# ReLU² attention and ReLU² MLP on one core: an earlier k load, a re-laid start of the MLP, two units' copies moved to VectorE, and a planner with shorter visits

## The chip, the cores and the metric

The kernel runs on one core of one Trainium2 chip. The metric is device time of one execution in microseconds (us). Nine runs of the kernel before had a median of 378.81 us and lay between 378.26 and 379.09 us. One further record is a profiled execution, whose instruction times are quoted throughout.

## The reference

The inputs are q, k and v of shape (8 batches, 12 heads, 448 rows, 64) and two weight matrices, all float32. What is computed:

```python
scores = (1/8) * q @ k.transpose
attn   = maximum(scores, 0)**2 / 448
x      = (attn @ v), heads side by side: 3584 tokens x 768
h      = x @ w_in                      # 768 -> 2048
g      = maximum(h, 0)**2
out    = g @ w_out                     # 2048 -> 768
```

There is no softmax, so a tile of attn needs only a relu with a scale (done by ScalarE out of PSUM) and a square (done by VectorE in SBUF).

## The kernel before

**Engines.** TensorE does all products, ScalarE (ACT) the relus of the scores and many evacuations of PSUM, VectorE (DVE) the squares, sums and other evacuations. GpSimd (POOL) issues the loads, which convert to float16 on the way; SP issues the DMA transposes and most stores. Each engine works through its instructions in the order in which the Python code emits them (`manual_schedule`).

**Attention.** Each batch is cut into three *units* of four heads (24 units in all), and each unit into seven *tiles* of 64 score columns per head (tile t belongs to unit t // 7). `score(t)` runs four 64x64 matmuls into a PSUM *slot*, and one ScalarE relu (line 256) empties it into an `at` tile, which VectorE squares (line 369). Two slots rotate, and a third exists in the first rounds only. When all seven tiles of a unit are squared, attn x v follows. For batch 0 this is `av_round`, tile by tile (line 270). For later units it is `av_unit`: 28 matmuls (line 317) and one ScalarE copy into `xt` (line 323).

**q and k, transposed.** Scores need q and k with the head dimension on the partitions. Units 0 to 5 are loaded as they are (`load16`) and transposed on TensorE by `pe_transpose(n)`: 28 small matmuls (line 222) into one slot, and two copies out of it, qT and kT. ScalarE makes these copies at line 214, VectorE at line 216: before the change VectorE for units 0 to 2, ScalarE for units 3 to 5. The slot is not free until both copies are done. Units 6 and up are transposed by DMA (`prefetch`).

**Visits.** A `visit` scores two tiles and queues their squares. In the first stage, 11 visits do the 21 tiles of batch 0, with each score run twice (`score(t, 2)`). After that, visits are *events*: each has a due time on a clock that only the matmul steps of the MLP advance, and it is emitted at the first step marked as an edge at which its time has come.

**MLP.** Batches 0 and 1 take plain products. `h_group(b, f)` is six matmuls of 448 columns (line 420, 0.1892 us each on the clock, so T_G = 1.135 us a group), then a relu by VectorE (line 429; batch 0, f = 0 and odd f below 14) or ScalarE (line 433), then `flush()`, which emits all squares that wait; after every odd group VectorE squares two columns of g (line 439). T_H, 16 groups, is the clock time at which batch 1 begins. Batches 2 to 7 (`h_period`, line 550) and the second product (`o_groups`, line 729) form 2x2 blocks with seven products instead of eight. They need sums of blocks, made by VectorE: `sums_w2` and `sums_w1` of the weights (lines 151 and 178 to 184), `sums_x`, and `sums` of g (line 602, called s1 to s4 below).

**The planner.** From batch 2 on, and in the second product, the order of VectorE's work comes from a model made while the code is emitted. `at_pe` is where TensorE would be, `at_ve` where VectorE would be. Squares go into a queue `due`, the relu and square of g into `due_g`, each with a time from which it is ready. `fill(until)` emits queued work that the model finishes before `until`; `now_ve(cost)` books an instruction that is emitted at once; `flush` empties the queues. `av_unit` flushes `due` ahead of its matmuls. A visit of two tiles counts as 0.19 + 0.38 * 2 = 0.95 us of TensorE, an `av_unit` as 2.65 us. These two figures change the order of VectorE's instructions alone: TensorE's steps follow the other clock.

**The seam.** Visit 11 scores tile 20, transposes unit 3 and does two tiles of attn x v. Then come four matmuls of group f = 0 (they need only units 0 and 1), the last three tiles of attn x v of batch 0, the first visit of batch 1, and the rest of the groups.

Of the kernel before, what the change touches and what calls it, by code (L numbers as in the profile page):

```python
# [12 lines left out]
AF = mybir.ActivationFunctionType  # L13
# [4 lines left out]
def kernel(  # L18
# [71 lines left out]
    def load16(n):  # L90
        tq = q16_p.tile([P, 2, J * D], FP16, name="q16", tag="q16")
        tk = q16_p.tile([P, 2, J * D], FP16, name="k16", tag="k16")
        nc.gpsimd.dma_start(out=tq, in_=heads(q, n))
        nc.gpsimd.dma_start(out=tk, in_=heads(k, n))
        q16s[n] = (tq, tk)

    def load_v(n):
        t = v_p.tile([P, 2, J * D], FP16, name="vt", tag="vt")
        nc.gpsimd.dma_start(out=t, in_=heads(v, n))
        vts[n] = t  # L100
# [44 lines left out]
    def sums_w2(i):  # L145


        op, c = divmod(i, 2)
        c = slice(4 * c, 4 * c + 4)
        dst, x, y = ((t1, b12, b11), (t3, b22, b12), (t2, b22, t1), (nt4, b21, t2))[op]  # L150
        nc.vector.tensor_sub(dst[:, c], x[:, c], y[:, c])
# [5 lines left out]
    nc.vector.memset(zeros, 0.0)  # L157
    junk = const_p.tile([P, 1], FP16, name="junk", tag="junk")
    nc.scalar.activation(out=junk, in_=zeros[:, 0:1], func=AF.Relu)
    load_v(0)  # L160
    load16(1)
    load_v(1)
    load16(2)
    load_v(2)

    def sums_w1(i):


        op, c = divmod(i, 2)
        now_ve(0.9)  # L170
        lo, hi = slice(0, NM // 2), slice(NM // 2, NM)
        a11, a12, a21, a22 = (w1[c][:, lo], w1[c][:, hi], w1[c + 2][:, lo],
                              w1[c + 2][:, hi])
        if op < 3:
            wsum[op, c] = late["ws"].tile(
                [P, NM // 2, 512], FP16, name=f"ws{op}{c}", tag=f"ws{op}{c}")
        if op == 0:
            nc.vector.tensor_add(wsum[0, c], a21, a22)
        elif op == 1:
            nc.vector.tensor_sub(wsum[1, c], wsum[0, c], a11)  # L180
        elif op == 2:
            nc.vector.tensor_sub(wsum[2, c], a12, wsum[1, c])
        else:
            nc.vector.tensor_sub(a21, a11, a21)
# [21 lines left out]
    def pe_transpose(n):  # L206
        srcs = q16s.pop(n)
        ts = new_qkt()
        ps = slot(FP16)

        def copy(i, eng):
            dst = ts[i].rearrange("p j c -> p (j c)")
            if eng == 0:
                nc.scalar.activation(out=dst, in_=pss[i][:, i, 0:J * P], func=AF.Copy)  # L214
            else:
                nc.vector.tensor_copy(dst, pss[i][:, i, 0:J * P])

        pss = [ps, slot(FP16) if n == 0 else ps]
        for i, src in enumerate(srcs):
            for j in range(J):  # L220
                for hh in range(2):
                    nc.tensor.transpose(  # L222
                        pss[i][64 * hh:64 * hh + 64, i, j * P:(j + 1) * P],
                        src[:, hh, j * D:(j + 1) * D], ident)
            if n == 0:
                copy(i, 1)
                warm(1)
        qkt[n] = ts
        if n == 3:
            return lambda: (copy(0, 0), copy(1, 0))  # L230
        if n > 0:
            copy(0, n < 3)
            copy(1, n < 3)
        return None


    xts: dict = {}
# [63 lines left out]
    def av_unit():  # L301

        n = unit[0]
        if n == NUN or seen.get(n * J + J - 1, 10 ** 6) >= now[0]:
            return
        unit[0] += 1
        flush(rest=False)
        at_pe[0] += 2.65
        b, u = divmod(n, NU)
        vt = vts[n]  # L310
        ps = slot(FP32)
        for j in range(J):
            at = ats.pop(n * J + j)
            for hp in range(2):
                r = slice(64 * hp, 64 * hp + 64)
                for hh in range(2):
                    nc.tensor.matmul(  # L317
                        ps[64 * hh:64 * hh + 64, hp, 0:S],
                        lhsT=vt[r, hh, j * D:(j + 1) * D], rhs=at[r, hh, :],
                        start=(j == 0), stop=(j == J - 1))  # L320
        if u == 0:
            xts[b] = x_p.tile([P, NM, S], FP16, name="xt", tag="xt")
        nc.scalar.activation(
            out=xts[b][:, 2 * u:2 * u + 2, :], in_=ps[:, :, 0:S],
            func=AF.Copy, scale=CX)
# [34 lines left out]
    def now_ve(cost, lag=0.25):  # L360
        at_ve[0] = max(at_ve[0], at_pe[0] + lag) + cost
# [9 lines left out]
    def visit(tiles, turn=None, lag=2, most=3):  # L371
        now[0] += 1
        for t in tiles:
            if t % J == 0 and t >= NPE * J:
                prefetch(t // J + 2)
        if big:
            for t in tiles[:1]:
                score(t)
            av_unit()
            for t in tiles[1:]:  # L380
                score(t)
            at_pe[0] += 0.19 + 0.38 * len(tiles)
            for i, t in enumerate(tiles):
                square(ats[t], 0.6 + 0.85 * i)
            return
        for t in tiles:
            score(t, 2)
        later = pe_transpose(turn) if turn is not None else None
        flush()
        av_some(lag, most)  # L390
        if later:
            later()
        for t in tiles:
            square(ats[t])
        flush()
# [16 lines left out]
    def h_group(b, f):  # L412
        z = (b % 2) * S
        cell = [None]

        def step(m):
            def run():
                if m == 0:
                    cell[0] = mm_tile()
                nc.tensor.matmul(  # L420
                    cell[0][:, 0:S],
                    lhsT=w1[f // 4][:, m, (f % 4) * P:(f % 4 + 1) * P],
                    rhs=xts[b][:, m, :], start=(m == 0), stop=(m == NM - 1))
                if m < NM - 1:
                    return
                f0 = f - f % 2
                g = g_of(b)[:, f0:f0 + 2, z:z + S]
                if b == 0 and (f % 2 == 1 or f == 0) and f < 14:
                    nc.vector.tensor_scalar(
                        out=g[:, f % 2], in0=cell[0][:, 0:S],  # L430
                        scalar1=0.0, scalar2=None, op0=ALU.max)
                else:
                    nc.scalar.activation(
                        out=g[:, f % 2], in_=cell[0][:, 0:S], func=AF.Relu)
                flush()
                if b == 0 and f == NF - 1:
                    square(g)
                elif f % 2 == 1:
                    nc.vector.tensor_mul(g, g, g)
            return run  # L440

        return [(0.1892, step(m), m == 0) for m in range(NM)]
# [151 lines left out]
    def sums(i, rows, to):  # L594

        a1, a2 = tile_of(rows[0]), tile_of(rows[1])
        x, y = ((a2[:, LO], a2[:, HI]), (to.get(1), a1[:, LO]),
                (a1[:, LO], a2[:, LO]), (a1[:, HI], to.get(2)))[i - 1]
        to[i] = late["s"].tile([P, KH, P], FP16, name=f"s{i}", tag=f"s{i}")
        op = nc.vector.tensor_add if i == 1 else nc.vector.tensor_sub  # L600
        now_ve(0.6)
        op(to[i], x, y)  # L602

# [170 lines left out]
    warm(10)  # L774
    pe_transpose(0)
    for i in range(11):
        visit([t for t in (2 * i, 2 * i + 1) if t < NB0],
              turn={1: 1, 4: 2, 10: 3}.get(i))
        if i == 0:
            load16(3)  # L780
            load_w1(0)
            load_w1(1)
            load_v(3)
        if i == 2:
            load16(4)
            load_w1(2)
            load_v(4)
        if i == 5:
            load16(5)
            load_w1(3)  # L790
            load_v(5)
    load_v(6)
    load_w2(b11, 0, 0)
    load_w2(b12, 0, 1)
# [2 lines left out]
    load_qk(6)  # L797
    load_qk(7)
    first.close()
    big.append(ctx.enter_context(tc.tile_pool(name="mma", bufs=2, space=PSUM)))  # L800


    f0 = h_group(0, 0)
    for _, fn, _ in f0[0:4]:
        fn()
    av_some(0, 9)
    rounds.close()
    big.append(ctx.enter_context(tc.tile_pool(
        name="mmb", bufs=2, space=PSUM, side="right", reuse_waits="tile")))
    visit([NB0, NB0 + 1])  # L810

    T_G = NM * 0.1892
# [20 lines left out]

    events.append((T_H + 0.2, ready))
    for i in range(8):
        events.append((T_H + (1 + i // 2) * T_G, lambda i=i: sums_w2(i)))
    for i in range(6):
        events.append((T_H + (8 + i) * T_G, lambda i=i: sums_w1(i)))
    for i in range(2):
        events.append((2 * T_H + 3 + 3 * i, lambda i=i: sums_w1(6 + i)))  # L840
    for m in (6, 7):
# [33 lines left out]
    for i in (1, 2):  # L875
        events.append((2 * T_H - (3 - i) * T_G, lambda i=i: outs[0][1](i)))

    steps = [(0.1892, None, False)] * 4 + f0[4:]
    for f in range(1, NF):
        steps += h_group(0, f)  # L880
    for f in range(NF):
        steps += h_group(1, f)
# [49 lines left out]
```

## Time and profile before

| | before |
|---|---|
| median of 9 runs | 378.81 us |
| the profiled execution's own time | 379.09 us |
| its span, first to last instruction | 377.3 us |
| TensorE matmul busy | 362.8 us (96%) |
| VectorE busy | 277.8 us (74%) |
| ScalarE busy | 249.8 us (66%) |
| GpSimd busy | 107.3 us (28%) |
| granted TensorE clock | 0.999 |

The span starts with the first instruction. 1.8 us of the profiled time lie outside it. Busy time of TensorE covers the whole passage of each matmul, so back-to-back matmuls overlap in it. The stages, by the start of their first matmul: transposes from 5.18 us, attention of batch 0 from 7.60, MLP groups of batch 0 from 27.69, the last attn x v of batch 1 (unit 5) at 58.76 and groups of batch 1 from about 61.6, the first second product from 84.11, then alternating `h_period` and `o_groups` to the last matmul at 372 us.

How lines of the views read: in a timeline, "12.35 4.96 ACT L256 ... x6 [0.79 <-PE slot L252]" means that from 12.35 us, for 4.96 us, ScalarE ran six instructions of line 256, and was idle for 0.79 us before them until TensorE's line 252 released it. In the list of waits, the three figures are total us, times, and the longest.

### The profile page before, as it was taken

How to read it: one execution, taken by the hardware profiler on the slowest of the kernel's cores; microseconds unless marked ns; L12 is line 12 of the kernel's file. 1: busy time of each engine (PE TensorE's matmuls, PEld its weight loads, DVE VectorE, ACT ScalarE, POOL GpSimd, SP SyncE). 2: the span in 40 equal slices, each digit the busy share in tenths (PEclk: the TensorE clock that was granted, in tenths of full speed). 3: DMA queues.
4: the chain of work that ended last, by engine and by line, in shares of the span. 5: the costliest groups of instructions: out<-in, count | busy, mean ns of one | idle time of the engine just before them, and what ended most of it. 6: DMA issues, size and time to landing. Idle time of an engine off the chain costs nothing.

```text
span 377.3 us, 8806 instructions
## 1 busy us (share of the span) xinstructions
PE 362.8 (96%) x3600; PEld 231.0 (61%) x3600; DVE 277.8 (74%) x515; ACT 249.8 (66%) x373; POOL 107.3 (28%) x128
## 2 busy tenths in 40 slices
PE   7889999999999999999999999999999999999994
PEld 3544444444455778785555577877555588985663
DVE  1886567997767688797865758989957688995542
ACT  2897995686777798775566578877766785532220
POOL 8545431927422436404041344050000000000001
PEclk9999999999999999999999999999999999999999
DMA  8999999999999999679498997693232200002333
GB/s 116 201 204 205 205 203 156 131 150 148 142 131 164 153 144 143 76 94 79 96 112 134 194 169 79 74 105 66 40 95 77 70 25 2 2 0 64 94 95 86
DMA packets 121160, 42.65 MB, mean 113 GB/s; under 512 B 100832, under 2 KB 117760, under 8 KB 121120
## 3 DMA queue, kind: packets, MB, share of 16 engines
q0 software_dynamic: 82912, 23.01, 60.6%
q1 hardware_dynamic: 38048, 18.98, 27.2%
q8 instruction: 28, 0.46, 0.5%
q14 instruction: 12, 0.10, 0.1%
q10 hardware_dynamic: 160, 0.10, 0.1%
HBM read 45.61 MB, written 11.01 MB: 150 GB/s over the span
## 4 chain that ended last, share of the span: by engine, by line
PE 82%; ACT 6%; DVE 6%; issue 2%; DMA 2%; POOL 1%; POOLq 0%; ACTq 0%; DVEq 0%
PE mm L729 33%; PE mm L550 23%; PE slot L252 9%; PE mm L420 9%; PE slot L317 7%; ACT at L256 4%; DVE at L369 2%; DMA k<-in_k_dram 2%; PE slot L222 1%; DVE g L491 1%; ACT m L486 1%; DVE xt L283 1%; DVE s L602 1%; DVE g L498 0%; ACT qT L214 0%
## 5 line engine op out<-in xcount | busy, mean ns | idle before, releaser
L256 ACT ACTIVATE at<-slot 128x896 f16<-128x896 f32 x168 | 146.1, 919 | 32.7 <-PE slot L252 32.7
L369 DVE TENSOR_TENSOR at<-at 128x896 f16<-128x896 f16 x168 | 99.8, 618 | 15.9 <-ACT at L256 14.8
L108 POOL DMA_DIRECT2D qs<-in_q_dram x36 | 35.3, 983 | 120.0 <-DMA qT<-qs 112.3
L729 PEld LDWEIGHTS <-s 128*128 128x128 f16 x440 | 41.7, 98 | 32.0 <-issue 4.3
L252 PE MATMUL slot<-qT,kT 64*64 64x448 f16 x756 | 58.1, 360 | 2.6 <-ACT at L256 1.2
L550 PEld LDWEIGHTS <-w 128*128 128x128 f16 x576 | 54.4, 98 | 5.9 <-issue 5.4
L550 PE MATMUL mm<-xt,w 128*128 128x224 f16 x432 | 48.6, 259 | 0.0
L729 PEld LDWEIGHTS <-g 128*128 128x128 f16 x336 | 31.5, 98 | 24.0 <-issue 5.0
L550 PEld LDWEIGHTS <-ws 128*128 128x128 f16 x432 | 40.2, 98 | 6.7 <-issue 6.7
L729 PE MATMUL mm<-b,g 128*128 128x384 f16 x224 | 40.7, 326 | 0.0
L420 PE MATMUL mm<-xt,w 128*128 128x448 f16 x192 | 39.6, 353 | 0.3 <-ACT xt L280 0.3
L729 PE MATMUL mm<-b,s 128*128 128x384 f16 x216 | 39.6, 326 | 0.1
L729 PE MATMUL mm<-t,s 128*128 128x384 f16 x224 | 39.5, 326 | 0.0
L636 DVE SCALAR_TENSOR_TENSOR osb<-mm,u 128x384 f32<-128x384 f32 (+1 forms) x30 | 16.2, 542 | 31.2 <-ACT u L631 23.0
L252 PEld LDWEIGHTS <-kT 64*64 64x64 f16 x756 | 20.0, 104 | 31.0 <-issue 25.7
L108 POOL DMA_DIRECT2D ks<-in_k_dram x36 | 35.3, 981 | 10.1 <-DMA b<-in_moe_w_out_dram 5.8
L571 POOL DMA_DIRECT2D out_dram<-osb x2 | 1.1, 563 | 120.4 <-DVE osb L636 120.4
L631 ACT ACTIVATE u<-mm 128x384 f32<-128x384 f32 x28 | 13.8, 492 | 32.6 <-PE mm L729 31.4
L550 PE MATMUL mm<-x,ws 128*128 128x224 f16 x288 | 34.4, 259 | 0.9 <-ACT m L486 0.9
L317 PE MATMUL slot<-at,vt 64*64 64x448 f16 x588 | 32.2, 350 | 0.6 <-DVE at L369 0.5
L498 DVE TENSOR_TENSOR g<-g 128x896 f16<-128x896 f16 x48 | 29.7, 619 | 1.1 <-ACT g L501 0.2
L420 PEld LDWEIGHTS <-w 128*128 128x128 f16 x192 | 17.3, 98 | 19.1 <-issue 4.8
(66 smaller groups left out, 398.4 us busy)
## 6 DMA issues: line engine op xcount, KB each, us to landing
out_dram<-osb SPq DMA_DIRECT2D x52, 192.0 KB, 3.3
vt<-in_v_dram POOLq DMA_DIRECT2D x24, 224.0 KB, 6.3
qs<-in_q_dram POOLq DMA_DIRECT2D x36, 112.0 KB, 4.8
ks<-in_k_dram POOLq DMA_DIRECT2D x36, 112.0 KB, 5.2
w<-in_moe_w_in_dram POOLq DMA_DIRECT2D x8, 384.0 KB, 12.0
b<-in_moe_w_out_dram POOLq DMA_DIRECT2D x4, 768.0 KB, 17.3
q<-in_q_dram POOLq DMA_DIRECT2D x6, 224.0 KB, 8.1
k<-in_k_dram POOLq DMA_DIRECT2D x6, 224.0 KB, 8.4
```

The source lines that it names most:

```text
L108: nc.gpsimd.dma_start(out=t[:, :, hh, :], in_=heads(src, n)[:, hh].rearrange("p (j d) -> p j d", d=D))
L222: nc.tensor.transpose(pss[i][64 * hh:64 * hh + 64, i, j * P:(j + 1) * P], src[:, hh, j * D:(j + 1) * D], ident)
L252: nc.tensor.matmul(ps[c, hh, 0:S], lhsT=kT[r, j, c], rhs=qT[r, :, c], start=True, stop=True)
L256: nc.scalar.activation(out=at, in_=ps[:, :, 0:S], func=AF.Relu, scale=SK)
L317: nc.tensor.matmul(ps[64 * hh:64 * hh + 64, hp, 0:S], lhsT=vt[r, hh, j * D:(j + 1) * D], rhs=at[r, hh, :], start=(j == 0), stop=(j == J - 1))
L369: lambda: nc.vector.tensor_mul(at, at, at), 0))
L420: nc.tensor.matmul(cell[0][:, 0:S], lhsT=w1[f // 4][:, m, (f % 4) * P:(f % 4 + 1) * P], rhs=xts[b][:, m, :], start=(m == 0), stop=(m == NM ...
L498: due_g.append((t, 0.54, lambda: nc.vector.tensor_mul(g, g, g), b))
L550: nc.tensor.matmul(XY[s][y][:, r * Q:(r + 1) * Q], lhsT=left(k, i0 + 2 * s + r, m), rhs=right(k, m), start=(fresh and r == 0 and m == 0), ...
L631: nc.scalar.activation(out=t, in_=X[0][:, 0:HALF], func=AF.Copy, scale=CO)
L636: nc.vector.scalar_tensor_tensor(out=osb[row][:, c], in0=acc[0][:, 0:cc.stop - cc.start], scalar=CO, in1=keep[nm][:, cc], op0=ALU.mult, op ...
L729: nc.tensor.matmul(acc[0][:, 0:HALF], lhsT=left()[:, f], rhs=right[:, f], start=(fresh and f == 0), stop=(f == KH - 1), skip_group_check=n ...
```

## The change

It does the following.

1. The first loads are issued as q and k of unit 1, v of unit 0, q and k of unit 2, v of units 1 and 2. Before, v of unit 0 came first and v of unit 1 between units 1 and 2.
2. `pe_transpose(3)` leaves visit 11 and comes right after it. Around the rest of attn x v of batch 0, the order is now: tiles 18 and 19, two matmuls of f = 0, the two copies of unit 3 (qT by ScalarE, kT by VectorE), tile 20, two more matmuls of f = 0, two of f = 1, the first visit of batch 1, and then the remaining matmuls of f = 1 and f = 0. The pool of the first two accumulators takes `reuse_waits="tile"`.
3. For units 4 and 5, VectorE makes both copies, after a `flush()`.
4. The planner counts 0.19 us a tile (0.57 for a visit of two) and 1.33 us an `av_unit`. Ahead of each `sums`, squares that the model takes as ready are emitted first.
5. `sums_w2(i)` is due at T_H + (2 + 0.75 i) T_G where it was T_H + (1 + i // 2) T_G; `sums_w1(i)` at T_H + (9 + 0.8 i) T_G where it was T_H + (8 + i) T_G.

```diff
@@ the first loads
+    load16(1)
     load_v(0)
-    load16(1)
+    load16(2)
     load_v(1)
-    load16(2)
     load_v(2)
...
@@ pe_transpose
         qkt[n] = ts
         if n == 3:
-            return lambda: (copy(0, 0), copy(1, 0))
+            return lambda: (copy(0, True), copy(1))
         if n > 0:
-            copy(0, n < 3)
-            copy(1, n < 3)
-        return None
+            flush()
+            copy(0)
+            copy(1)
...
@@ av_unit
-        at_pe[0] += 2.65
+        at_pe[0] += 1.33
...
@@ visit
-            at_pe[0] += 0.19 + 0.38 * len(tiles)
+            at_pe[0] += 0.19 + 0.19 * len(tiles)
...
-        later = pe_transpose(turn) if turn is not None else None
+        if turn is not None:
+            pe_transpose(turn)
         flush()
         av_some(lag, most)
-        if later:
-            later()
...
@@ sums
+        while due and due[0][0] <= max(at_ve[0], at_pe[0]) + 0.3:
+            put(due)
         now_ve(0.6)
         op(to[i], x, y)
...
@@ the seam
-        visit([t for t in (2 * i, 2 * i + 1) if t < NB0],
-              turn={1: 1, 4: 2, 10: 3}.get(i))
+        visit([t for t in (2 * i, 2 * i + 1) if t < NB0], turn={1: 1, 4: 2}.get(i))
...
+    later = pe_transpose(3)
     load_v(6)
...
-    big.append(ctx.enter_context(tc.tile_pool(name="mma", bufs=2, space=PSUM)))
+    big.append(ctx.enter_context(tc.tile_pool(
+        name="mma", bufs=2, space=PSUM, reuse_waits="tile")))
...
-    f0 = h_group(0, 0)
-    for _, fn, _ in f0[0:4]:
-        fn()
+    f0, f1 = h_group(0, 0), h_group(0, 1)
...
+    av_some(1, 9)
+    some(f0[0:2])
+    later()
     av_some(0, 9)
     rounds.close()
...
+    some(f0[2:4])
+    some(f1[0:2])
     visit([NB0, NB0 + 1])
...
-        events.append((T_H + (1 + i // 2) * T_G, lambda i=i: sums_w2(i)))
+        events.append((T_H + (2 + 0.75 * i) * T_G, lambda i=i: sums_w2(i)))
...
-        events.append((T_H + (8 + i) * T_G, lambda i=i: sums_w1(i)))
+        events.append((T_H + (9 + 0.8 * i) * T_G, lambda i=i: sums_w1(i)))
...
-    steps = [(0.1892, None, False)] * 4 + f0[4:]
-    for f in range(1, NF):
+    steps = [(0.1892, None, False)] * 6 + f1[2:4] + f0[4:6] + f1[4:6]
+    for f in range(2, NF):
         steps += h_group(0, f)
```

More of the change, by code (lines that the diff above doesn't have):

```diff
@@ L209, in pe_transpose, with copy @@
         ps = slot(FP16)
[L211 to L214, printed above, removed]
+        def copy(i, act=False):
+            dst, ps = ts[i].rearrange("p j c -> p (j c)"), pss[i][:, i, 0:J * P]
+            if act:
+                nc.scalar.activation(out=dst, in_=ps, func=AF.Copy)
             else:
-                nc.vector.tensor_copy(dst, pss[i][:, i, 0:J * P])
+                nc.vector.tensor_copy(dst, ps)
         pss = [ps, slot(FP16) if n == 0 else ps]
@@ L225, in pe_transpose @@
             if n == 0:
-                copy(i, 1)
+                copy(i)
                 warm(1)
@@ L799, with some @@
     first.close()
-    big.append(ctx.enter_context(tc.tile_pool(name="mma", bufs=2, space=PSUM)))
-    f0 = h_group(0, 0)
-    for _, fn, _ in f0[0:4]:
-        fn()
+    big.append(ctx.enter_context(tc.tile_pool(
+        name="mma", bufs=2, space=PSUM, reuse_waits="tile")))
+    f0, f1 = h_group(0, 0), h_group(0, 1)
+    def some(part):
+        for _, fn, _ in part:
+            fn()
+    av_some(1, 9)
+    some(f0[0:2])
+    later()
     av_some(0, 9)
```

## The prediction

> **What bounds the kernel.** I read the page first: shares, then slices.
>
> ```profile
> PE 362.8 (96%) x3600; PEld 231.0 (61%) x3600; DVE 277.8 (74%) x515; ACT 249.8 (66%) x373; POOL 107.3 (28%) x128
> ...
> PE   7889999999999999999999999999999999999994
> ```
>
> TensorE is the bound, and only its idle time is to be had: 14.5 us of the 377.3, about 5 of them after the last matmul. The change takes no matmul away. So I asked next for whom TensorE waits:
>
> ```profile
> PE slot L222 <- DMA k<-in_k_dram: 0.9, 2, 0.6
> ...
> PE mm L550 <- ACT m L486: 0.9, 3, 0.4
> ...
> PE mm L550 <- DVE g L491: 0.7, 2, 0.3
> ...
> PE slot L252 <- ACT kT L214: 0.5, 2, 0.3
> PE slot L317 <- DVE at L369: 0.5, 2, 0.4
> ```
>
> No wait is large; each edit has to be followed to its own wait. The timelines of the stages that are touched (TensorE, ScalarE and VectorE rows):
>
> ```profile
> 11.22 0.58 PE L222 MATMUL slot<-ident,k 128*64 128x128 f16 x14 [0.64 <-DMA k<-in_k_dram]
> ...
> 12.35 4.96 ACT L256 ACTIVATE at<-slot 128x896 f16<-128x896 f32 x6 [0.79 <-PE slot L252]
> ...
> 26.28 0.58 PE L222 MATMUL slot<-ident,q 128*64 128x128 f16 x14 [0.57 <-ACT at L256]
> ...
> 29.94 2.81 PE L420 MATMUL mm<-xt,w 128*128 128x448 f16 x14 [0.25 <-ACT xt L280]
> ...
> 34.53 0.62 DVE L429 TENSOR_SCALAR g<-mm 128x448 f16<-128x448 f32 x1 [1.13 <-PE mm L420]
> 35.08 1.15 DVE L369 TENSOR_TENSOR at<-at 128x896 f16<-128x896 f16 x2
> 36.14 0.61 DVE L439 TENSOR_TENSOR g<-g 128x896 f16<-128x896 f16 x1
> ...
> 35.44 0.92 ACT L214 ACTIVATE qT<-slot 128x896 f16<-128x896 f16 x1 [0.49 <-PE slot L222]
> 36.26 0.91 ACT L214 ACTIVATE kT<-slot 128x896 f16<-128x896 f16 x1
> ...
> 37.22 0.38 PE L252 MATMUL slot<-qT,kT 64*64 64x448 f16 x4 [0.26 <-ACT kT L214]
> ```
>
> Up to 27 us ScalarE sets the pace (0.82 us from one relu of line 256 to the next), from 28 us on TensorE does, with short waits for slots. The VectorE rows matter most: after a group with odd f (here f = 3) it has four instructions in hand, g, two squares and g squared, before it could copy anything.
>
> **Part 1, the loads.** Transfers land one after the other: q and k of unit 0 at 5.13 and 6.26 us, v of unit 0 at 8.20, q and k of unit 1 at 9.32 and 11.18, then v at 12.26. With v moved behind, q of unit 1 takes v's place (8.20) and k lands at 9.32, or at 10.15 if the long step of 1.86 us belongs to it. The transposes of q run 10.00 to 10.41 (they wait for a slot), those of k follow to 10.90, tile 4's score ends at 10.90 + 0.57 = 11.47. The relu of tile 3 starts at 10.63, so the next can start at 10.63 + 0.82 = 11.45: 11.5 instead of 12.35, **-0.85**. The three issues swap places in GpSimd's queue, 0.7 each, with no wait among them before 11.46. v lands at 11.18, and its first reader (line 270, 12.51 before) comes at 11.7. v of units 1 and 2 lands at 14.6 and 15.7, used at 19 and 24. The stage is paced by ScalarE up to 27 us, so the shift is carried on whole; later loads keep their places and have over 1 us of slack at every reader. Bounds: 0 (another wait takes its place) and -0.9 (all of the gap).
>
> **Part 2, the seam.** Times from here on are those of before, part 1 left out. The two tiles of attn x v of visit 11 (8 matmuls, 0.37 us) come ahead of the transposes and so fall into the 0.57 us wait for a slot, which still ends at 26.28. After the transposes (27.19): 0.50 (tiles 18, 19) + 0.48 (2 matmuls of f = 0) + 0.22 (tile 20) + 0.86 (4) + 0.50 (visit) + 2.37 (12 matmuls to the end of f = 2) = 4.93, so 32.12; before it was 32.68. The wait of 0.25 for xt at 29.94 goes because four matmuls cover it. VectorE's kT copy runs from 27.7 to 28.3, behind the square of tile 20, and the visit needs it at 29; the accumulators of f = 0 were not waited for before, so `reuse_waits` is put at nothing. **-0.56**; bounds -0.2 (one new wait, for the kT copy, at the first visit) and -0.8 (both idles).
>
> **Part 3, copies of units 4 and 5.** TensorE waits in the second score of the next visit for the slot to come free. Before: f = 3 ends at 34.43, transposes 0.91, two ScalarE copies, score at 37.22, 2.74 to the last copy's end at 37.17. After, counted from the same end: 0.10 to the start of g, 0.55 + 1.06 + 0.54 for g, two squares and g squared (the starts above), 0.54 for qT and 0.62 for kT = 3.41. `flush()` adds nothing, since each group has flushed. So +0.66 a unit: in exchange ScalarE is relieved of 1.63 us, and the next visit no longer waits for its relus (tiles 27 and 28: 0.82 from start to start against 0.50 for a visit without a wait, -0.32). Followed through: -0.56 at the end of f = 3; +0.10 at the score; -0.24 at the end of f = 7; unit 5 the same, +0.40 at its score; -0.32, +0.08. There the last squares of unit 4 end 3.40 us after f = 9, while TensorE would now reach the seventh tile of `av_unit` after 3.07: the 0.32 comes back, +0.40. So **+0.96** for part 3, and parts 2 and 3 together +0.40.
> The Trainium skill speaks for this edit: "ScalarE: Activation LUTs", Rules for kernel authors, has VectorE rather than ScalarE for simple element-wise work, and "Perfetto Trace Analysis", Optimizing Scalar/DVE Operations, says a VectorE mode makes it faster, but not where VectorE is saturated. By the first alone, each pair of copies would end earlier and the part would gain. The rows decide: a copy takes 0.62 us at line 216 against 0.92 at line 214, but it stands fifth in its queue.
> Bounds: VectorE free when the transposes end, 35.44 + 0.54 + 0.62 = 36.60 against 37.17, so -0.57 a unit and -0.3 for the relieved visit, -1.7 in all; and +1.5 if no visit is relieved.
>
> **Part 4, sums of the weights.** From 62.4 us VectorE is the fuller engine:
>
> ```profile
> 62.40:86.00 23.60, 23.29 (x35) 1.00 1.73 143
> ```
>
> (of 23.60 us, 23.29 busy). Its row at 62.97 is `sums_w2`, two of the eight, 0.87 each, emitted at group 1. After the change the first stands at group 2, behind the square of groups 0 and 1, which needs ScalarE's relu (64.06 + 0.54 = 64.60). So VectorE stands idle from 62.97 to 64.62, 1.65 us, and everything behind it up to the square of tile 48 (same work, save s1) ends 1.65 later. The `av_unit` of unit 6 starts at 82.50 and needs tile 48 at 83.63; that square ended at 83.31, 0.32 ahead. The new rule in `sums` lets it go ahead of s1 (0.60): the planner has `at_ve` ahead by two bookings of 0.9 at group 13. 1.65 - 0.32 - 0.60 = **+0.73**. Who waits behind it: s1 and s2, 0.6 each, needed only at 88. Bounds: 0 (TensorE late by other causes) and +1.33 (s1 first).
>
> **Part 5, the planner.** The trace has 0.50 us for a visit and 1.32 for 28 matmuls, so the new figures are the truer ones; VectorE looks fuller to the model, and squares and `due_g` go out later, evacuations earlier. What there is to win: the waits for `DVE g L491` stand behind a ScalarE copy that has two relus in front of it, not behind a square (152.57, two relus; 154.18 m; 154.77 g). Of the waits for `DVE at L369`, the large one (0.92 us lost at 92.2) has its squares behind an evacuation emitted before any `fill` could place them; that order stays. About 0.3 is to be won. To lose: read from the rows, 5 of the 17 later units have their last square less than 1 us ahead of need. Two squares left to the flush in `av_unit` take 1.07 from TensorE's arrival, and it needs the last after 0.21 + 1.12 = 1.33; one evacuation of 0.62 in front costs 0.36. Two such cases: **+0.2** net. Bounds -0.5 and +2.0 (six units at 0.36).
>
> **Sum.** -0.85 - 0.56 + 0.96 + 0.73 + 0.2 = +0.48. The profiled execution took 379.09 (377.3 span and 1.8 around it), so 379.57; it stands 0.28 above the median of 378.81, so 379.3. 0.2% is 0.76 us, about what a measurement of this kernel can tell from no change.
>
> **Rivals.** *The lead is kept* (faster): VectorE reaches the two copies as the transposes end, part 3 at -1.7, or the stall of part 4 is covered. For it: ScalarE's copies are on the chain that ends last, and its relus wait behind them. Against it: the four VectorE rows above. With part 3 at 0 and part 4 at 0, -0.85 - 0.56 + 0.2 = -1.2, so 377.6; with part 3 at its bound, 375.9. It decides once kT's copy ends before about 36.5 on the times of before.
> *Squares come late* (slower): the truer planner leaves the last two squares of a unit to the flush in `av_unit`. For it: the small margins; against it: `fill` takes squares ahead of `due_g`. At 0.36 to 0.6 for eight units, +3 to +5 less what part 5 had: about 382. It overtakes the rest from three units on.
> *Nothing reaches the end*: later stages wait for ScalarE anyway (121.85, 150.90, 220.66, 237.38 and 253.09 have ScalarE as releaser), but these waits are fixed to TensorE's steps, so a shift passes through them whole. Time as before, 378.8.
>
> **How the numbers follow.** The sum as worked out, 0.50: range 378.3 to 380.3, so 0.02 faster, 0.28 same, 0.20 slower. The kept lead, 0.26: 0.24 faster, 0.02 same. Late squares, 0.17: all slower. Nothing, 0.07: same. Together faster 0.26, same 0.37, slower 0.37. 377.5 leaves out the lower part of the kept lead, 381.0 most of the late squares, one in ten each.
>
> **What would show it.** Part 1: no 0.79 in front of the third visit's relus, first MLP matmul of f = 2 over 0.8 us earlier. Part 2: no waits at the transposes of unit 3 beyond 0.25 and none for xt. Part 3: VectorE copies directly behind line 439, TensorE idle over 0.5 us in front of two scores, released by kT. Part 4: VectorE idle after 63 us, TensorE waiting for line 369 in unit 6. Wrong would be: kT's copies ahead of the squares, no stall at unit 6, or several new stalls at line 317 after 100 us.

## The result and the profile after

The changed kernel has a median of 380.68 us over 9 runs (380.56 to 380.91), against 378.60 us for the kernel before on the same chip (29 runs; the 378.81 quoted ahead is the median of the first nine): slower by 2.08 us, a ratio of 1.0056 with a 95% interval from 1.0047 to 1.0064. Its profiled execution took 380.60 us with a span of 378.8 us, so the two profiled executions differ by 1.5 us, 0.5 less than the medians. The kernel before's profiled execution (379.09) lies at the top of its runs, the changed kernel's (380.60) near the middle of its own; all that follows about places is read between these two traces.

In the changed kernel the line numbers of the MLP are one lower (L419, L549) or one higher (L730, L603) than before. The page's busy times, and the list of whom TensorE waits for (total us, times, longest):

```profile
PE 363.7 (96%) x3600; PEld 231.0 (61%) x3600; DVE 281.6 (74%) x520; ACT 245.9 (65%) x368; POOL 107.2 (28%) x128
```

```profile
PE slot L252 <- DVE kT L216: 2.3, 3, 0.9
PE slot L317 <- DVE at L369: 1.4, 4, 0.6
...
PE mm L549 <- ACT m L485: 0.9, 3, 0.4
...
PE mm L730 <- DVE s L603: 0.2, 1, 0.2
```

ScalarE did five instructions fewer and VectorE five more. The waits for k's load and for ScalarE's kT are gone from the list. At its head stand VectorE's kT copies (before: 0.4 for one) and squares that attn x v waits for (before: 0.5, twice); a wait for a sum s is new. The waits behind ScalarE's m copies are what they were, 0.9.

The surest way to read where time went is to pair every matmul of one trace with the same matmul of the other, and to see where the difference of their start times changes. There are seven such places (the figures are running totals):

| place | difference after minus before |
|---|---|
| third visit, 11 us | -0.85 |
| end of the seam (visit of tiles 23 and 24) | -1.30 |
| second score behind unit 4's transposes | -0.64 |
| second score behind unit 5's transposes | -0.01 (-0.06 at the next attn x v, -0.01 from 52 us on) |
| unit 6, last tile of attn x v | +0.80 |
| product with s3, 212.7 us | +1.18 |
| unit 20, last tile of attn x v | +1.55, kept to the end |

So the lead of 1.30 us was real, and lost by 47 us. Timelines of the changed kernel at these places. First TensorE and VectorE behind group f = 3, with the transposes of unit 4 ending at 34.03:

```profile
33.23 0.62 DVE L428 TENSOR_SCALAR g<-mm 128x448 f16<-128x448 f32 x1 [0.37 <-PE mm L419]
33.78 1.15 DVE L369 TENSOR_TENSOR at<-at 128x896 f16<-128x896 f16 x2
34.84 0.62 DVE L438 TENSOR_TENSOR g<-g 128x896 f16<-128x896 f16 x1
35.38 0.62 DVE L216 COPY qT<-slot 128x896 f16<-128x896 f16 x1
35.91 0.61 DVE L216 COPY kT<-slot 128x896 f16<-128x896 f16 x1
...
36.58 0.38 PE L252 MATMUL slot<-qT,kT 64*64 64x448 f16 x4 [0.93 <-DVE kT L216]
```

VectorE has no idle time between the five rows: the copies are not slow, they are fifth in line, and TensorE waits 0.93 us for the last. Next, the start of unit 3's `av_unit`, TensorE and ScalarE:

```profile
39.88 0.38 PE L252 MATMUL slot<-qT,kT 64*64 64x448 f16 x4
40.35 1.52 PE L317 MATMUL slot<-at,vt 64*64 64x448 f16 x28
...
38.57 1.73 ACT L256 ACTIVATE at<-slot 128x896 f16<-128x896 f32 x2 [0.64 <-PE slot L252]
```

The four matmuls at 39.88 need 0.21 us (40.83 to 41.04 before), but attn x v starts 0.47 later, 0.05 after ScalarE's second relu ended at 40.30. `av_unit` takes a slot too, and the slot was still full. Third, VectorE behind 62 us, and TensorE in unit 6:

```profile
62.36 0.62 DVE L369 TENSOR_TENSOR g<-g 128x896 f16<-128x896 f16 x1 [2.29 <-ACT g L432]
64.63 0.63 DVE L438 TENSOR_TENSOR g<-g 128x896 f16<-128x896 f16 x1 [1.64 <-ACT g L432]
65.17 1.82 DVE L151 TENSOR_TENSOR t<-b,b 128x1536 f16<-128x1536 f16 x2
...
83.76 1.15 DVE L369 TENSOR_TENSOR at<-at 128x896 f16<-128x896 f16 x2
84.83 0.68 DVE L603 TENSOR_TENSOR s<-g 128x1024 f16<-128x1024 f16 x1
...
84.43 0.38 PE L317 MATMUL slot<-at,vt 64*64 64x448 f16 x4 [0.64 <-DVE at L369]
```

The idle 1.64 us is new, the squares at 83.76 now precede s1 at 84.83, and TensorE still waits 0.64. In the kernel before `sums_w2` filled that gap, and unit 6's 28 matmuls ran through:

```profile
62.97 1.82 DVE L151 TENSOR_TENSOR t<-b,b 128x1536 f16<-128x1536 f16 x2
...
82.50 1.49 PE L317 MATMUL slot<-at,vt 64*64 64x448 f16 x28
```

Fourth, VectorE and TensorE at the two places that the prediction did not have:

```profile
210.60 0.62 DVE L369 TENSOR_TENSOR at<-at 128x896 f16<-128x896 f16 x1 [0.72 <-ACT at L256]
211.40 0.62 DVE L369 TENSOR_TENSOR at<-at 128x896 f16<-128x896 f16 x1 [0.18 <-ACT at L256]
211.94 0.68 DVE L603 TENSOR_TENSOR s<-g,g 128x1024 f16<-128x1024 f16 x1
...
212.69 1.47 PE L730 MATMUL mm<-b,s 128*128 128x384 f16 x8 [0.20 <-DVE s L603]
...
272.58 0.61 DVE L497 TENSOR_TENSOR g<-g 128x896 f16<-128x896 f16 x1
273.11 0.38 DVE L495 TENSOR_SCALAR g<-g 128x896 f16<-128x896 f16 x1
273.53 0.63 DVE L497 TENSOR_TENSOR g<-g 128x896 f16<-128x896 f16 x1
274.07 1.16 DVE L369 TENSOR_TENSOR at<-at 128x896 f16<-128x896 f16 x2
...
274.75 0.38 PE L317 MATMUL slot<-at,vt 64*64 64x448 f16 x4 [0.19 <-DVE at L369]
```

At 211 the new rule in `sums` lets s3 wait for two squares whose relus have only just ended. At 272 three pieces of `due_g` (lines 495 and 497) go ahead of the squares that unit 20 needs. In the kernel before, s3 went ahead of those two squares, and the first of the three squares at 272.52 was the one that unit 20 needed at 273.19:

```profile
208.97 0.68 DVE L602 TENSOR_TENSOR s<-g,g 128x1024 f16<-128x1024 f16 x1
...
272.52 1.69 DVE L369 TENSOR_TENSOR at<-at 128x896 f16<-128x896 f16 x3
```

### The profile page after: what moved, and what is told of

Read it like the earlier page. It is cut to its first block, busy times and chain, and to the rows that moved or that the text cites. A ratio compares the mean times of both kernels' runs of the same rounds, so it can differ in the third digit from the quotient of the medians.

```text
span 378.8 us, 8798 instructions
## 1 busy us (share of the span) xinstructions
PE 363.7 (96%) x3600; PEld 231.0 (61%) x3600; DVE 281.6 (74%) x520; ACT 245.9 (65%) x368; POOL 107.2 (28%) x128
## 4 chain that ended last, share of the span: by engine, by line
PE 74%; DVE 14%; ACT 6%; issue 3%; DMA 1%; POOL 0%; POOLq 0%; ACTq 0%; DVEq 0%
PE mm L730 31%; PE mm L549 23%; PE slot L252 8%; PE slot L317 7%; ACT at L256 5%; PE mm L419 4%; DVE at L369 4%; DMA k<-in_k_dram 1%; DVE g L497 1%; DVE g L438 1%; DVE s L603 1%; ACT m L485 1%; DVE t L151 1%; PE slot L222 1%; DVE g L490 1%
## 5 line engine op out<-in xcount | busy, mean ns | idle before, releaser
L730 PEld LDWEIGHTS <-s 128*128 128x128 f16 x440 | 41.6, 98 | 32.4 <-issue 3.5
L549 PEld LDWEIGHTS <-w 128*128 128x128 f16 x576 | 54.4, 98 | 5.9 <-issue 5.4
L549 PE MATMUL mm<-xt,w 128*128 128x224 f16 x432 | 48.6, 259 | 0.0
L730 PEld LDWEIGHTS <-g 128*128 128x128 f16 x336 | 31.5, 98 | 24.2 <-issue 5.2
L549 PEld LDWEIGHTS <-ws 128*128 128x128 f16 x432 | 40.2, 98 | 6.7 <-issue 6.7
L730 PE MATMUL mm<-b,g 128*128 128x384 f16 x224 | 40.7, 326 | 0.0
L730 PE MATMUL mm<-b,s 128*128 128x384 f16 x216 | 39.6, 326 | 0.3 <-DVE s L603 0.2
L419 PE MATMUL mm<-xt,w 128*128 128x448 f16 x192 | 39.8, 354 | 0.0
L730 PE MATMUL mm<-t,s 128*128 128x384 f16 x224 | 39.5, 326 | 0.0
L549 PE MATMUL mm<-x,ws 128*128 128x224 f16 x288 | 34.4, 259 | 0.9 <-ACT m L485 0.9
L490 DVE TENSOR_TENSOR g<-mm,m 128x448 f16<-128x448 f32 x36 | 22.1, 620 | 9.7 <-ACT m L485 4.1
```

The source lines that it names most:

```text
L419: nc.tensor.matmul(cell[0][:, 0:S], lhsT=w1[f // 4][:, m, (f % 4) * P:(f % 4 + 1) * P], rhs=xts[b][:, m, :], start=(m == 0), stop=(m == NM ...
L490: nc.vector.tensor_add(gs(s, hi, right), acc(s, y), keep[s, nm])
L549: nc.tensor.matmul(XY[s][y][:, r * Q:(r + 1) * Q], lhsT=left(k, i0 + 2 * s + r, m), rhs=right(k, m), start=(fresh and r == 0 and m == 0), ...
L730: nc.tensor.matmul(acc[0][:, 0:HALF], lhsT=left()[:, f], rhs=right[:, f], start=(fresh and f == 0), stop=(f == KH - 1), skip_group_check=n ...
```

## The experiments

Each was timed in five rounds against the kernel before on its own chip. "Place shift" is read by pairing the matmuls of two traces, as above: the difference of their start times, or how far it moves at a place. Where a text sets a median beside that of the changed kernel, the two come from different rounds, in which the kernel before had 378.60 and 378.78 to 378.86 us; 0.2 to 0.3 us of such a difference can be the rounds', and the place shift is the better figure.

| run | median, us | the kernel before there | ratio, 95% interval | span |
|---|---|---|---|---|
| e1_load | 378.30 | 378.86 | 0.9984, 0.9976 to 0.9993 | 376.5 |
| e2_act45 | 379.41 | 378.86 | 1.0010, 0.9993 to 1.0026 | 377.9 |
| e3_times | 379.80 | 378.86 | 1.0027, 1.0018 to 1.0037 | 378.0 |
| e6_copies_first | 378.53 | 378.86 | 0.9987, 0.9978 to 0.9997 | 376.9 |
| e4_old_costs | 380.34 | 378.78 | 1.0035, 1.0022 to 1.0047 | 378.6 |
| e5_no_loop | 382.72 | 378.78 | 1.0096, 1.0072 to 1.0119 | 380.5 |
| e7_act_old_rest | 377.89 | 378.78 | 0.9972, 0.9958 to 0.9986 | 376.0 |
| e8_first_old_rest | 376.96 | 378.78 | 0.9945, 0.9924 to 0.9965 | 375.2 |
| e10_times_alone | 380.37 | 378.82 | 1.0040, 1.0028 to 1.0052 | 378.7 |
| e11_copies_alone | 380.24 | 378.82 | 1.0042, 1.0026 to 1.0057 | 380.8 |
| e9_squares_first | 376.02 | 378.82 | 0.9929, 0.9917 to 0.9941 | 374.2 |

**e1_load: the loads alone.** The kernel before, with:

```diff
-    load_v(0)
     load16(1)
-    load_v(1)
+    load_v(0)
     load16(2)
+    load_v(1)
```

> The kernel before with part 1 alone (unit 1's q and k loaded ahead of v). Theory (each wait has its own price and shifts are carried on by TensorE): the 0.8 us gap in front of the third visit's relus goes, nothing takes its place, later stages move as a whole: span 377.3 - 0.85 = 376.4, time 0.85 below before. Rival (the gain is lost again at the seam, as the whole lead was in the changed kernel, where TensorE stood at -0.01 us by unit 5): no difference, within 0.2 us.

The gap in front of the third visit's relus is closed:

```profile
9.09 7.45 ACT L256 ACTIVATE at<-slot 128x896 f16<-128x896 f32 x9
16.88 1.73 ACT L256 ACTIVATE at<-slot 128x896 f16<-128x896 f32 x2 [0.34 <-PE slot L252]
```

Nine relus without a break. Every matmul from 14 us on is 0.71 to 0.78 earlier, the span by 0.8. The medians show 0.56, with an interval of 0.3 to 0.9. So the shift is carried through the whole kernel, as the theory had it, and the rival, no more than 0.2, falls; the 0.2 between trace and medians comes back below.

**e2_act45: the changed kernel with ScalarE's copies of units 4 and 5.**

```diff
-            copy(0)
-            copy(1)
+            copy(0, n > 3)
+            copy(1, n > 3)
```

> The changed kernel, but ScalarE copies units 4 and 5 again. Theory (the VectorE copies stand behind four instructions and end 0.66 us later from the end of the group; the visits' relus are no gain, since av_unit's slot waits for them): TensorE keeps -1.3 us at both units, so 1.3 below the changed kernel, 379.4 against 380.7. Rival (ScalarE's relus are what the stage waits for, so with ScalarE loaded again about as much is lost): within 0.4 us of the changed kernel.

379.41 us, 1.27 below the changed kernel. In the trace the two waits for kT are 0.26 again, as before, and the place shift against the changed kernel goes from +0.50 to -0.79 past unit 4's attn x v, 1.29 in all. (The +0.50 is there from 8 us on. It is not a late load: q and k of unit 0 landed at 5.13 and 6.25 us, against 5.14 and 6.23, but their 14 transposes each took 0.96 and 0.81 us, against 0.73 and 0.58. 0.96 us is what 14 such transposes took at half the clock in e11, see the last section, but that the clock was the cause here is not shown.) ScalarE's relief was no gain.

**e6_copies_first: same engine, another place in its queue.** The changed kernel, where behind groups 3 and 7 the flush of squares and the square of g are held until the copies are emitted:

```diff
-                flush()
-                if b == 0 and f == NF - 1:
+                def rest():
+                    flush()
...
+                if b == 0 and f in (3, 7):
+                    held.append(rest)
...
-            flush()
             copy(0)
             copy(1)
+            while held:
+                held.pop()()
```

> The changed kernel, but behind groups 3 and 7 VectorE makes the two copies ahead of the squares and of the square of g. Theory (place in VectorE's queue, not the engine, is what costs): copies end about 2.2 us after the group instead of 3.4, when TensorE reaches the score after 2.34, so the two waits of 0.93 us vanish; 1.4 to 2.1 us below the changed kernel, depending on how much returns at later slots. Rival (the squares now come late and av_unit of unit 3 or 4 waits for them instead): less than 0.5 us below.

378.53 us, 2.15 below the changed kernel (place shift from +0.24 to -1.89, 2.13 in all). VectorE, and TensorE's next two visits:

```profile
33.47 0.62 DVE L430 TENSOR_SCALAR g<-mm 128x448 f16<-128x448 f32 x1 [0.37 <-PE mm L421]
34.38 0.62 DVE L216 COPY qT<-slot 128x896 f16<-128x896 f16 x1 [0.28 <-PE slot L222]
34.92 0.61 DVE L216 COPY kT<-slot 128x896 f16<-128x896 f16 x1
35.45 1.15 DVE L370 TENSOR_TENSOR at<-at 128x896 f16<-128x896 f16 x2
...
35.51 0.57 PE L253 MATMUL slot<-qT,kT 64*64 64x448 f16 x8
...
37.83 0.38 PE L253 MATMUL slot<-qT,kT 64*64 64x448 f16 x4 [0.20 <-ACT at L257]
```

The copies end at 35.53 and the visit at 35.51 runs its eight matmuls without a stop. What is left is a wait of 0.20 for a relu. e2 shows that part 3 cost the time; e6, with the same instructions on the same engine, that the cost was their place: it takes three of the four instructions ahead of the copies out of their way.

**e11_copies_alone: part 3 on the kernel before.**

```diff
-            copy(0, n < 3)
-            copy(1, n < 3)
+            copy(0, 1)
+            copy(1, 1)
```

> The kernel before with units 4 and 5 copied by VectorE, nothing else. Theory (0.66 us a unit by the place in the queue, and what the relieved relus give comes back at av_unit's slot): 1.3 us above before. Rival (as the prediction had it, 0.3 of a unit's loss is kept from the relieved visit, once): 1.0 above.

1.42 us above before. In its profiled execution k of unit 1 landed late (12.29 us where it was 11.18) and the kernel ran 2.19 behind from 15 us on; from there to the score behind unit 4's attn x v the shift grew to 3.48, by 1.29: +0.66 at the first score that waits for kT, -0.29 at the relieved visit, +0.23 at `av_unit`, and nearly the same again for the next unit. That is the theory's 1.3, and no visit's relief was kept. The medians alone do not decide against the rival's 1.0: their interval is 1.0 to 2.2.

**e3_times and e10_times_alone: the due times of the weight sums.** e3 is the changed kernel with the due times of before, e10 the kernel before with the new ones:

```diff
-        events.append((T_H + (1 + i // 2) * T_G, lambda i=i: sums_w2(i)))
+        events.append((T_H + (2 + 0.75 * i) * T_G, lambda i=i: sums_w2(i)))
...
-        events.append((T_H + (8 + i) * T_G, lambda i=i: sums_w1(i)))
+        events.append((T_H + (9 + 0.8 * i) * T_G, lambda i=i: sums_w1(i)))
```

> The changed kernel with the due times of sums_w2 and sums_w1 of before. Theory (VectorE's idle 1.64 us behind the square at 62.36 is what makes tile 48's square late): no wait in unit 6's av_unit, 0.8 us below the changed kernel. Rival (the new planner or the shifted seam makes unit 6 late): the wait of 0.64 us stays, time as the changed kernel within 0.2 us.

> The kernel before with the later due times of sums_w2 and sums_w1 alone. Theory (1.65 us of idle time put into VectorE's full stretch, 0.32 of it covered; without the new rule s1 also stays ahead of tile 48's square): unit 6's av_unit waits 1.3 us more than before, time 1.35 above before. Rival (it costs only together with the new planner): within 0.3 us of before.

e3: 379.80 us, 0.88 below the changed kernel, with a place shift of 0.81 in unit 6. Unit 6's 28 matmuls run through, without a wait:

```profile
82.60 1.49 PE L317 MATMUL slot<-at,vt 64*64 64x448 f16 x28
```

e10: 1.55 above before; the only change of place shift is +1.41 in unit 6:

```profile
85.04 0.38 PE L317 MATMUL slot<-at,vt 64*64 64x448 f16 x4 [1.24 <-DVE at L369]
```

So the due times cost this by themselves, and the new rule in `sums`, which e10 lacks, had hidden 0.6 of it in the changed kernel (1.41 against 0.81).

**e4_old_costs and e5_no_loop: the two halves of the planner.** e4 is the changed kernel with 2.65 and 0.38 put back, e5 the changed kernel without the rule:

```diff
-        while due and due[0][0] <= max(at_ve[0], at_pe[0]) + 0.3:
-            put(due)
         now_ve(0.6)
```

> The changed kernel with the planner's costs of before (0.38 a tile, 2.65 an av_unit), the new rule in sums kept. Theory (the new costs hold back due_g, whose backlog is emitted ahead of the squares of unit 20; the wait for s3 at 212.69 comes from the rule in sums): the wait at 274.75 goes back to that of before, 212.69 and unit 6 stay; 0.3 to 0.4 us below the changed kernel. Rival (costs without effect, both waits come from the rule): as the changed kernel within 0.15 us.

> The changed kernel without the new rule in sums, new costs kept. Theory (the rule puts two squares ahead of s3, which costs 0.37 at 212.69, but it also puts tile 48's square ahead of s1, which saves 0.6 in unit 6): the wait for s3 goes, the wait in unit 6 grows from 0.64 to about 1.25; 0.2 us above the changed kernel. Rival (the rule only delays): 0.4 us below.

e4: 0.34 below the changed kernel, and the place shift of -0.28 comes at unit 20 alone, whose last square now has 0.75 us to spare. The waits at unit 6 and at s3 stay. e5 missed: 2.04 above the changed kernel instead of 0.2. Two of its three parts came as expected (unit 6 waits 1.24, the wait for s3 is gone); the third was unit 20. VectorE and TensorE there:

```profile
272.89 0.61 DVE L497 TENSOR_TENSOR g<-g 128x896 f16<-128x896 f16 x1
273.42 0.38 DVE L495 TENSOR_SCALAR g<-g 128x896 f16<-128x896 f16 x1
273.84 0.62 DVE L497 TENSOR_TENSOR g<-g 128x896 f16<-128x896 f16 x1
274.50 0.69 DVE L601 TENSOR_TENSOR s<-g 128x1024 f16<-128x1024 f16 x1
275.23 0.69 DVE L601 TENSOR_TENSOR s<-s,g 128x1024 f16<-128x1024 f16 x1
275.84 1.69 DVE L369 TENSOR_TENSOR at<-at 128x896 f16<-128x896 f16 x3
...
276.51 0.38 PE L317 MATMUL slot<-at,vt 64*64 64x448 f16 x4 [1.64 <-DVE at L369]
```

The backlog of `due_g` and then both sums go ahead of the squares. So without the rule the new costs lose about 1.8 us at unit 20, and the rule takes most of it back; as a pair they cost 0.75 at s3 and unit 20 together.

**e7_act_old_rest and e8_first_old_rest: the useful parts together.** Both are the changed kernel with the due times and the planner of before; e7 has ScalarE's copies as in e2, e8 VectorE's copies ahead of the squares as in e6.

> Parts 1 and 2 alone: the early k and the new seam (unit 3's kT by VectorE), with ScalarE's copies of units 4 and 5, and the due times and the planner of before. Theory (prices add up: -0.8 for the loads, -0.45 for the seam, and nothing takes it back without parts 3 to 5): 1.25 us below before, and both unit 6's wait and those at 212 and 274 of the changed kernel absent. Rival (the lead meets a fixed wait): 0.8 below, as the loads alone.

> Parts 1 and 2, units 4 and 5 copied by VectorE ahead of the squares, due times and planner of before. Theory: the loads 0.8, the seam 0.45, and 0.7 to 0.9 from the copies, which no longer hold the slots: 1.95 to 2.2 us below before, 376.7. Rival (with TensorE so far ahead, VectorE's chain of sums after 62 us makes unit 6 late): about 1.4 below, with a wait for line 370 in unit 6.

e7: 0.89 below before, span 1.3 below, place shift -1.28 at the seam and -1.25 at the end: the lead of parts 1 and 2 is kept once parts 3 to 5 are out. The medians again show some 0.4 less than the traces, and by them alone the rival's 0.8 would fit better than the theory's 1.25; that the place shift moves by no more than 0.03 behind the seam speaks against it. e8: 1.82 below before, a little less than expected (place shift -2.07), 0.9 better than e7, with no wait in unit 6.

**e9_squares_first: one step on.** e8, and in `end7` of the second product:

```diff
                 copy("u3")
+                while due and due[0][0] <= max(at_ve[0], at_pe[0]) + 0.3:
+                    put(due)
                 plus(1, c1, "u3")
```

> The best so far (early k, new seam, VectorE's copies of units 4 and 5 ahead of the squares, due times and planner of before), and in end7 of the second product the ready squares are emitted ahead of the evacuation. Theory (the two waits of unit 7 come from squares that stand behind an evacuation which waits for ScalarE): both waits for line 370 near 92 us go, 0.9 us less, 376.1. Rival (other evacuations come late for it and TensorE waits for an accumulator): no gain.

376.02 us, 2.80 below before and 0.94 below e8 (place shift 1.03 at unit 7), the best of all. VectorE and TensorE at unit 7, first in e8, where the evacuation waits 1.50 us ahead of the squares, then in e9:

```profile
90.51 0.56 DVE L642 SCALAR_TENSOR_TENSOR osb<-mm,u 128x384 f32<-128x384 f32 x1 [1.50 <-ACT u L637]
90.99 1.15 DVE L370 TENSOR_TENSOR at<-at 128x896 f16<-128x896 f16 x2
...
91.66 0.38 PE L318 MATMUL slot<-at,vt 64*64 64x448 f16 x4 [0.37 <-DVE at L370]
```

```profile
89.20 0.62 DVE L370 TENSOR_TENSOR at<-at 128x896 f16<-128x896 f16 x1 [0.31 <-ACT at L257]
90.01 0.62 DVE L370 TENSOR_TENSOR at<-at 128x896 f16<-128x896 f16 x1 [0.18 <-ACT at L257]
90.56 0.55 DVE L642 SCALAR_TENSOR_TENSOR osb<-mm,u 128x384 f32<-128x384 f32 x1
...
90.03 1.52 PE L318 MATMUL slot<-at,vt 64*64 64x448 f16 x28
```

The squares use the time in which the evacuation would only have waited for ScalarE, and the 28 matmuls run through.

## Why the prediction was right or wrong

The forecast was 379.3 us, a loss of 0.5, and "same" as likely as "slower"; measured were 380.68 and a loss of 2.08. The range, up to 381.0, held it, in part by luck: the sum as worked out was allowed 378.3 to 380.3, and what carried the range further was the rival of late squares, whose mechanism gave only 0.37 us of the loss, at unit 20. The direction of the sum was right and its size a quarter of what came. Step by step, from the traces:

| step | predicted | measured | shown by |
|---|---|---|---|
| part 1, loads | -0.85 | -0.85 | e1: -0.8 in the span |
| part 2, seam | -0.56 | -0.45 | e7: -1.28 with part 1 |
| part 3, copies | +0.96 | +1.29 | e11: +1.29, e2: -1.29, e6 more than undoes it |
| part 4, weight sums | +0.73 | +0.81 | e3: -0.81; e10 |
| part 5, planner | +0.2 | +0.75 | e4, e5 |
| sum | +0.48 | +1.55 | spans 377.3 and 378.8 |

*Part 1* was right, with the mechanism. *Part 2* was right but for the term of tile 20: 0.31 us between its first matmul and the next group's, where 0.22 was put in. No run has `reuse_waits` alone, which was put at nothing.

*Part 3* was right in its mechanism and in the 0.66 a unit (from the end of the group to the second score 3.45 us against 2.79, at both units). The step that failed is the visit relieved of its wait for relus, -0.32, which the working kept for unit 4 and gave back only for unit 5, to late squares. Measured, it was -0.29 at both units and came back at both, nearly all of it at the next `av_unit`, whose own slot waits for the same relus (0.26 at 39.88). With no visit relieved, 0.66 twice is 1.32 (the prediction wrote +1.5 for that bound); measured were 1.29. Its own terms, added up without a slip, also give +1.00 and not +0.96: 0.10 - 0.32 is -0.22, not -0.24, and 0.66 more is +0.44, not +0.40. The rule weighed there (the Trainium skill, "ScalarE: Activation LUTs", Rules for kernel authors: VectorE rather than ScalarE for `relu`, `max`, `min`, `add` and `mul`) speaks of the speed of an instruction, and there the rows agree for these copies too, 0.62 us against 0.92. Read as a rule on where to put work it would have had this part gain, and e11 lost 1.42 us; with the copies second in the queue VectorE did gain, 0.9 in e8 against e7.

*Part 4* came as worked out: 1.64 idle against 1.65, the squares ahead of s1 as the planner's figures said, 0.81 lost against 0.73. e10 without the rule lost 1.41 against a bound of 1.33. Most of the 0.08 that both are over is a term left out of the margin of 0.32: TensorE started 0.05 to 0.06 us after the end of the square that it waited for (84.43 after 84.38, and in e10 85.04 after 84.98).

*Part 5* was too small: +0.2 against +0.75. First, its own terms give more than it wrote: two cases at 0.36 less the 0.3 to be won are +0.42. None of the 0.3 was won; no place shift goes down behind 52 us. Then two costs came that it did not have in the form they took. The rule in `sums` was priced at the one place where it helps (unit 6), and not at s3, where it costs 0.38: s3 is needed by the product after next, and two squares with their relus take just longer. And the loss at `av_unit` was put down to evacuations standing in front of squares in several units; it came at one, unit 20 (+0.37), whose last square had ended only 0.05 us ahead of need (273.14 for 273.19), by `due_g` that the truer costs had held back. e4 takes 0.28 of it back, and e5 shows how large it is without the rule. The rival *squares come late* named this mechanism, at eight units; it decided at one. *The lead is kept* fell in the changed kernel, by exactly the four VectorE rows held against it. With three of them behind the copies and the old due times and planner, in e8, the lead stays and grows (-2.07). *Nothing reaches the end* fell: shifts pass through all later stages, as every place shift shows.

The remaining 0.5 us of the difference between the medians is not in the two traces. In the experiments too, but for e2 and for e11 with its late load, the spans put a kernel 0.1 to 0.4 us better against the kernel before than the medians do (0.7 in e5, whose profiled execution, 382.28, was itself 0.44 below its median). That fits a profiled execution of the kernel before that was itself 0.2 to 0.5 slow (379.09, with medians of 378.60 to 378.86 in the comparisons); where it lost that is open.

## What to carry to other kernels

When work moves to an engine that is idle on average, count what stands ahead of it in that engine's queue at that moment: here a faster instruction came 0.66 us later, and two pairs of the same instruction, each three places earlier, gained 2.13 us between the traces. The idle time put into a stretch where VectorE was 99% busy came out at the far end, less the margin that its consumer had. A planner that is made truer can still be slower, where the order under the old figures happened to fit; read the margins (0.05 us at unit 20) before changing it, and pair the matmuls of the two traces to see where a lead goes.

## What was not expected of the hardware

The landing of the first loads varies between executions by more than the whole effect of some edits: k of unit 1 landed at 11.18 us in the profiled execution of the kernel before and at 12.29 in that of e11, with the same issue times within 0.02 us, and TensorE waited 0.64 and 1.74 us for it:

```profile
12.33 0.96 PE L222 MATMUL slot<-ident,k 128*64 128x128 f16 x14 [1.74 <-DMA k<-in_k_dram]
```

The 1.11 us of the late load became 2.19 us by 15 us, since TensorE also ran slower behind the longer wait. The profile's granted TensorE clock is 0.50 of full speed from 12.3 to 15.6 us in that execution, and 1.00 in the same stretch before, behind the wait of 0.64 us. The 14 transposes took 0.96 us where they took 0.58. Whether the length of the wait is what brought the clock down was not tested: no other trace here has such a drop between its first loads and its last matmul.

With the early load, k of unit 1 landed between 8.96 and 9.41 us in all ten profiled executions that have it. In the changed kernel it landed at 9.38, 0.99 us ahead of its use at 10.37, so that a delay like that of e11 would be hidden but for about 0.1 us (an estimate, 1.11 less 0.99). This was not seen in a run.
